# The prologue of a clustered attention and MoE kernel: the first head pair's masks built head by head

## The chip, the cores and the metric

The kernel runs on one core of one Trainium2 chip. The metric is the device time of one execution in microseconds. The profile is that of one execution, by the hardware profiler.

## The reference

Three parts follow one another: an attention in which a query sees only the keys of its own cluster, a dense MLP, and a mixture of experts with a skip rule. The change lies in the attention, in its first microseconds.

```python
B, H, S, D = 2, 8, 768, 64                 # centroids: (8, 16, 64)
q_n, k_n, c_n = (t / (norm(t) + 1e-6) for t in (q, k, centroids))
q_assign = argmax(einsum('bhsd,hcd->bhsc', q_n, c_n), -1)
k_assign = argmax(einsum('bhsd,hcd->bhsc', k_n, c_n), -1)
mask = q_assign[..., :, None] == k_assign[..., None, :]
scores = where(mask, q @ k.T / sqrt(D), -1e9)
attn = softmax(scores) @ v                  # (2, 8, 768, 64)
x = attn as (1536, 512); h = x @ w_in; x = max(0.01 * h, h) @ w_out
# then: top-1 expert of 8 for each token with x @ w_skip > 0, added to x
```

## The kernel before

**Tiling.** The 16 heads are worked on as 8 pairs (`p`), two heads side by side in the 128 partitions. A pair takes 12 steps `s` of the main loop: 6 query tiles of 128 for each of 2 heads; even steps are head 0, odd steps head 1. In a step, `st_scores` makes a 128x768 score tile on TensorE (tile `sps`) and takes its row maximum on VectorE (`st`); `st_exp` takes the exponential on ScalarE (`pr`); three steps later `st_transpose` and `st_evac` turn the tile (`tps`, evicted to `pt` by ScalarE, L435); later still `st_av` multiplies by v. Score tiles use a PSUM tag S of two buffers.

**Precision and masks.** A score is a sum of two pairs of matmuls (L371). q and k are split into a rounded `hi` part and a rest `lo`. For head 0, tile `UA` holds hi in rows 0 to 63 and the one-hot cluster of each query (times a big constant, minus it) and key in rows 64 to 79; it is used with 80 rows. Tile `VA` holds a second arrangement of hi and lo in 128 rows. Head 1 has `UB` and `VB`. Each tile has a q half (index 0) and a k half (index 1). Since the transposed pair has head 1 in partitions 64 to 127, and V needs hi and lo across the halves, parts of U and V are copied between partitions by DMA, 192 KB each ("exchange" transfers).

**Prologue (pair 0).** `load_qk(0)` loads q, the centroids (`cnat`, L107) and k, and `load_qk(1)` the next pair, all on SyncE's queue (SP). `first_copy(i)` regroups a half of q or k, one head on ScalarE (L475), the other on VectorE for q (L477) and GpSimd (POOL) for k (L479). `prep_centroids` normalises the centroids on VectorE into `cexp`; `prep_cblk` transposes them (L164). `raw_pe` transposes q and k (L179) and `raw_act` evicts them (L191). `first_hi` makes hi: q on POOL (L199), k on ScalarE (L197); `first_lo` makes lo on VectorE (L497). Then come the exchange transfers of pair 0: L502 to L505 (hi), L509 (head 1's lo of q, read from VA rows 64 to 127 of the q half), L510 (on POOL's queue), L514 and L515 (lo of k), and last

```python
nc.sync.dma_start(Yq[0:64], Xq[64:128])     # L509: VB <- VA
...
nc.sync.dma_start(Xq[64:128], Uq[0:64])     # L516: VA <- UA, over the rows that L509 reads
```

`assign_pe` multiplies by the centroids (`asps`, L232), `assign_act` evicts (`sc`, L238), `argmax_pe` transposes the scores of both heads, q and k, into one tile of 128x384 (`scps`, L244). `argmax_0` to `argmax_3` are five VectorE operations on that whole tile (L251, L256, L259, L264, L269) that end in the one-hot `oh`. Then `raw_pe` and `raw_act` of pair 1 are issued, and `mask_first(0)` and `mask_first(1)`: 12 transposes of `oh` each (`mps`, L280), k's part evicted by ScalarE (L283), q's by VectorE (L286). `split_first(1, i)` (POOL, L208 and L209) and its DMAs follow, then the loop.

**Order.** The schedule is written by hand: each engine executes in the order in which the program issues to it, and the framework adds the semaphores. A DMA waits on its queue's engine before it is issued, and holds what stands behind it there.

Of the kernel before, what the change touches and what calls it, by code (L numbers as in the profile page):

```python
# [8 lines left out]
F32 = mybir.dt.float32  # L9
F32R = mybir.dt.float32r  # L10
F16 = mybir.dt.float16
BF16 = mybir.dt.bfloat16
I32 = mybir.dt.int32
U32 = mybir.dt.uint32
AF = mybir.ActivationFunctionType
# [10 lines left out]
def kernel(  # L26
# [42 lines left out]
    def ps_s(name):  # L69
        return psum.tile([P, 2, 512], F32, tag="S", name=name, bufs=2)  # L70
# [4 lines left out]
    def ps_a(shape, name, dt=F32):  # L75
        return psum.tile(shape, dt, tag="A", name=name, bufs=1)
# [16 lines left out]
    def load_qk(p):  # L93
        b, cc = divmod(p, NPAIR)
        for nm, src in (("q", q), ("k", k)):
            if p:
                t = att_a.tile([P, NT, 2, D], F32, tag="nat" + nm, name="nat" + nm)
                nat[nm, p] = t
                nc.sync.dma_start(t, src[b, 2 * cc:2 * cc + 2].rearrange("h (p t) d -> p t h d", t=NT))
            else:  # L100
                t = att.tile([P, 2, HS], F32R, tag="pr", name="first", bufs=4)
                t = _f(t.rearrange("p a b -> p (a b)")).rearrange("p (h t d) -> p h t d", h=2, d=D)
                nc.sync.dma_start(t, src[b, 0:2].rearrange("h (p t) d -> p h t d", t=NT))
                first[nm] = t
                nat[nm, 0] = nat0[:, "qk".index(nm)]
            if p == 0 and nm == "q":
                nc.sync.dma_start(cnat, centroids.rearrange("h c d -> (h c) d"))  # L107

    def load_v(p):
        b, cc = divmod(p, NPAIR)  # L110
# [51 lines left out]
    def prep_cblk():  # L162
        cps = ps_s("cps")[:, 0, 0:P]
        nc.tensor.transpose(cps, cexp.rearrange("p h d -> p (h d)"), ident)  # L164
        nc.vector.tensor_copy(cblk.rearrange("p a b -> p (a b)"), cps)
# [5 lines left out]
    def raw_pe(p, i):  # L171
        if i == 0:
            raw_t[p] = att_a.tile([P, 4, HS], F32, tag="raw", name="raw")
            uv_t[p] = tuple(att_a.tile([P, 2, S], F32R, tag=n, name=n, bufs=2) for n in ("UA", "UB", "VA", "VB"))
        qk, half = divmod(i, 2)
        src = nat["qk"[qk], p]
        ps = ((ps_t, ps_t, ps_m, ps_a)[i] if p == 0 else ((ps_t, ps_t, ps_a, ps_t)[i] if p == 1 else ps_m))([P, 3, P], "rawps")
        for j in range(3):
            nc.tensor.transpose(ps[:, j, :], src[:, 3 * half + j].rearrange("p h d -> p (h d)"), ident)  # L179
        ps_prep["raw", i] = ps  # L180
# [89 lines left out]
                                op=ALU.is_equal)  # L270
        oh_t[p] = oh

    def mask_first(h):
        U = uv_t[0][h]
        for qk in (1, 0):
            ps = (ps_m if h else ps_t)([P, S], "mps", BF16) if qk or not h else ps_a([P, S], "mps", BF16)
            for i in range(2):
                for j in range(3):
                    o = (3 * i + j) * P
                    nc.tensor.transpose(ps[64:64 + NC_, o:o + P], oh_t[0][:, j, 4 * qk + 2 * i + h, :], identb)  # L280
            ps = ps[64:64 + NC_, :]
            if qk:
                nc.scalar.activation(out=U[64:64 + NC_, 1, :], in_=ps, func=AF.Copy)  # L283
            else:
                for cs in (slice(0, HS), slice(HS, S)) if h == 0 else (slice(0, S),):
                    nc.vector.tensor_scalar(out=U[64:64 + NC_, 0, cs], in0=ps[:, cs], scalar1=BIG, scalar2=-BIG,  # L286
                                            op0=ALU.mult, op1=ALU.add)

    def mask_pe(p):
        ps = ps_m([P, 3, P], "ohps", BF16)  # L290
# [178 lines left out]
    def first_copy(i):  # L469
        nm = "qk"[i // 2]  # L470
        ts_ = slice(3 * (i % 2), 3 * (i % 2) + 3)
        for h in range(2):
            src, dst = first[nm][:, h, ts_, :], nat[nm, 0][:, ts_, h, :]
            if h:
                nc.scalar.activation(out=dst, in_=src, func=AF.Copy)  # L475
            elif nm == "q":
                nc.vector.tensor_copy(dst, src)  # L477
            else:
                nc.gpsimd.tensor_scalar(out=dst, in0=src, scalar1=1.0, scalar2=1.0, op0=ALU.mult, op1=ALU.mult)  # L479

    first_copy(0)
    prep_centroids()
    first_copy(2)
# [10 lines left out]
    def first_lo(qk, halves=(0, 1)):  # L494
        for half in halves:
            cs = slice(half * HS, (half + 1) * HS)
            nc.vector.tensor_tensor(out=lo_k[:, half, :] if qk else VA[:, 0, cs], in0=raw_t[0][:, 2 * qk + half, :],  # L497
                                    in1=_f(UA[:, qk, cs]), op=ALU.subtract)
# [6 lines left out]
    nc.sync.dma_start(Yk[0:64], Uk[64:128])  # L505
    first_lo(0, (0,))
    prep_cblk()
    first_lo(0, (1,))
    nc.sync.dma_start(Yq[0:64], Xq[64:128])  # L509
    nc.gpsimd.dma_start(Xk[0:64], Uk[0:64])  # L510
    assign_pe(0)
    first_lo(1)
    lo_kf = _f(lo_k.rearrange("p a b -> p (a b)"))
    nc.sync.dma_start(Xk[64:128], lo_kf[0:64])  # L514
# [2 lines left out]
    prep(0, 3, "a0")  # L517
    nc.scalar.activation(out=warm, in_=warm, func=AF.Exp)
    prep(0, 3, "pb")
    for r in range(4, 7):  # L520
        for slot in ("d", "pb"):
            prep(0, r, slot)
    load_v(0)
    for i in range(4):
        raw_pe(1, i)
        raw_act(1, i)
    load_qk(2)
    mask_first(0)
    mask_first(1)
    for i in range(4):  # L530
        split_first(1, i)

# [149 lines left out]
    def conv_ops(n, a, b):  # L682
        if 0 <= n < len(pieces):
            for i_ in range(a, b):
                convert_op(*pieces[n], i_)
            if b == 5:
                load_next(n + 5)

    for s in range(NSTEP + 12 + LAG):
        p, r = divmod(s, 12)  # L690
        if s < NSTEP:
            st_scores(s)
        conv_step(s, 0)
        preps(p, r, "a0")
        preps(p, r, "pa")
        if 0 <= s - LAG < NSTEP:
            st_transpose(s - LAG)
            st_evac(s - LAG)
        gf, rf = divmod(s, 6)
        if 0 < gf <= NSTEP // 6:  # L700
            if rf == 3:
                recip_rows(gf - 1)
            elif rf == 4:
                nc.sync.dma_start(rscr[gf - 1], rrow_t.pop(gf - 1))
        g, kt = divmod(s - 6 - LAG, 6)
        if 0 <= g < NSTEP // 6 and kt % 2:
            st_av(g, kt - 1)
            st_av(g, kt)
        if s < NSTEP:
            st_exp(s)  # L710
        if 0 <= g < NSTEP // 6 and kt == NT - 1:
            av_evac(g)
            av_split(g)
        if 0 <= g < NSTEP // 6 and kt == 3:
            recip_load(g)
        if 0 < gf <= NSTEP // 6 and rf < 2:
            recip(gf - 1, rf)
        preps(p, r, "d")
        preps(p, r, "pb")
        if r == 10 and p + 1 < NP:  # L720
            load_v(p + 1)
        conv_step(s, 1)
        if s == NSTEP:
            att_a.release()
            rt = pool("rt", "left")
            ring_b[0] = pool("ring_b", "left")
            wip[0] = pool("wi", "left")
            for c in range(NDIR // 4, NPC // 4):
                load_f32(c)
            load_next(2)  # L730
        if s == NSTEP + 4:
            for i in range(3):
                split_i(i)
# [848 lines left out]
```

## Time and profile before

| | us |
|---|---|
| median of 3 runs | 661.1 (661.08 to 661.39) |
| the profiled execution | 660.89 |
| its span in the trace | 659.2 |
| first matmul in the trace | 4.41 |
| first score matmuls | 18.08 |

The profile's times count from the start of the span. "Busy" is time in which an engine executes; what stands in brackets behind an instruction is how long its engine was idle before it and what ended the wait. The chain of waits follows from the last instruction back to what released it each time. A row "x4" merges instructions of one kind that follow each other.

### The profile page before, as it was taken

To read this page: it belongs to the slowest core of one execution; us is meant where nothing else is said; L and a number is where in the kernel's file an instruction comes from. 1 tells how busy PE (TensorE), PEld (TensorE's weight loads), DVE (VectorE), ACT (ScalarE), POOL (GpSimd) and SP (SyncE) were. 2 spreads that over 40 slices of the span, in tenths; PEclk is the share of its full clock that TensorE was granted. 3 is DMA by queue.
4 is the path that set the end of the run, shared out by engine and by line. 5 is a ranking of instruction groups with operands and counts; after the bars stand their busy time and mean duration, and the time that the engine had idled before them with its cause. 6 is when DMAs were issued, how large, how long until landed. Compare 5 with 4: busy or idle time off the path is not lost.

```text
span 659.2 us, 10058 instructions
## 1 busy us (share of the span) xinstructions
PE 632.9 (96%) x3599; PEld 489.3 (74%) x3599; DVE 437.8 (66%) x767; ACT 422.5 (64%) x829; POOL 164.2 (25%) x215
## 2 busy tenths in 40 slices
PE   5999989999999999999999999999999999999995
PEld 4766666766776765888888888888888878688874
DVE  6756668686768663898865335645556548999962
ACT  5887787988888886655454444444654356688860
POOL 4234636463727324400000000000000025004211
PEclk9999999999999999999999999999999999999998
DMA  8865655667675617232104000006145337999930
GB/s 193 202 175 144 157 142 150 171 185 191 182 193 137 181 46 271 75 125 95 34 1 167 25 0 1 1 0 256 39 155 190 138 128 254 365 369 366 372 133 27
DMA packets 63636, 99.53 MB, mean 151 GB/s; under 512 B 27697, under 2 KB 31763, under 8 KB 63200
## 3 DMA queue, kind: packets, MB, share of 16 engines
q1 hardware_dynamic: 60304, 90.62, 44.1%
q0 software_dynamic: 3280, 8.24, 3.8%
q8 instruction: 29, 0.48, 0.3%
q14 instruction: 23, 0.19, 0.1%
HBM read 72.73 MB, written 12.70 MB: 130 GB/s over the span
## 4 chain that ended last, share of the span: by engine, by line
PE 87%; ACT 6%; DVE 3%; issue 2%; POOL 2%; DMA 0%; POOLq 0%
PE ups L669 20%; PE acc L775 19%; PE sps L371 9%; PE avps L443 9%; PE hps L1273 7%; PE yps L1304 7%; PE tps L428 7%; ACT pr L389 2%; ACT pt L435 2%; DVE st L374 1%; PE hT L1285 1%; PE acc L1165 1%; PE x2T L859 1%; PE rawps L179 1%; PE asps L232 1%
## 5 line engine op out<-in xcount | busy, mean ns | idle before, releaser
L374 DVE TENSOR_REDUCE st<-sps 128x1 f32<-128x768 f32 x96 | 91.7, 955 | 69.0 <-PE sps L371 68.5
L435 ACT ACTIVATE pt<-tps 128x384 f32<-128x384 f32 x192 | 84.6, 501 | 25.8 <-PE tps L428 25.0
L389 ACT ACTIVATE pr<-sps,st 128x768 f32<-128x768 f32 x96 | 87.2, 909 | 10.9 <-DVE st L374 10.3
L428 PE MATMUL tps<-ident,pr 128*128 128x128 f32 x576 | 78.6, 272 | 0.5 <-ACT pt L435 0.5
L669 PE MATMUL ups<-xh,whii 128*128 128x512 f32 x192 | 74.8, 390 | 0.0
L669 PE MATMUL ups<-xh,wloi 128*128 128x512 f32 x192 | 74.7, 389 | 0.0
L669 PE MATMUL ups<-xl,whii 128*128 128x512 f32 x192 | 74.7, 389 | 0.0
L775 PE MATMUL acc<-whio,gh 128*128 128x512 f32 x183 | 73.0, 399 | 0.0
L443 PE MATMUL avps<-pt,vnat 128*64 128x384 f32 x384 | 72.1, 498 | 0.0
L428 PEld LDWEIGHTS tps<-ident,pr 128*128 128x128 f32 x576 | 68.2, 140 | 5.1 <-ACT pt L435 1.6
L775 PE MATMUL acc<-whio,gl 128*128 128x512 f32 x183 | 71.4, 390 | 0.0
L775 PE MATMUL acc<-wloo,gh 128*128 128x512 f32 x183 | 71.3, 390 | 0.0
L760 ACT ACTIVATE gh<-g 128x512 fp32r<-128x512 f32 x48 | 30.4, 633 | 43.6 <-DVE g L759 43.6
L758 ACT ACTIVATE lk<-ups 128x512 f32<-128x512 f32 x48 | 28.4, 592 | 37.3 <-PE ups L669 30.8
L759 DVE TENSOR_TENSOR g<-ups,lk 128x512 f32<-128x512 f32 x48 | 33.0, 688 | 28.7 <-ACT lk L758 28.6
L762 DVE TENSOR_TENSOR gl<-g,gh 128x512 fp32r<-128x512 f32 x48 | 33.3, 693 | 25.2 <-ACT gh L760 25.2
L1013 POOL DMA_INDIRECT xe<-x_scratch,eix x1 | 1.2, 1165 | 190.0 <-DVE eix L1012 190.0
L646 DVE TENSOR_TENSOR wloi<-rawb,whii 128x512 fp32r<-128x512 f32 x36 | 24.7, 686 | 27.5 <-ACT whii L645 27.4
L443 PEld LDWEIGHTS avps<-pt,vnat 128*64 128x64 f32 x384 | 23.4, 136 | 25.6 <-issue 25.5
L669 PEld LDWEIGHTS ups<-xh,whii 128*128 128x128 f32 x192 | 36.0, 188 | 8.1 <-issue 0.6
L669 PEld LDWEIGHTS ups<-xl,whii 128*128 128x128 f32 x192 | 36.1, 188 | 7.5
L669 PEld LDWEIGHTS ups<-xh,wloi 128*128 128x128 f32 x192 | 36.0, 188 | 7.4
(303 smaller groups left out, 1350.1 us busy)
## 6 DMA issues: line engine op xcount, KB each, us to landing
rawb<-in_moe_w_dram SPq DMA_DIRECT2D x25, 1024.0 KB
rawa<-in_moe_w_dram SPq DMA_DIRECT2D x10, 1024.0 KB
stg<-in_moe_w_in_dram SPq DMA_DIRECT2D x16, 512.0 KB
stg<-in_moe_w_out_dram SPq DMA_DIRECT2D x16, 512.0 KB
UB<-UA SPq DMA_DIRECT2D x16, 192.0 KB
vnat<-in_v_dram SPq DMA_DIRECT2D x8, 384.0 KB
rb<-recip_scratch POOLq DMA_DIRECT2D x32, 96.0 KB, 2.9
w_f_scratch<-cvt SPq DMA_DIRECT2D x12, 256.0 KB
```

Source lines behind the costliest of these rows:

```text
L371: nc.tensor.matmul(ps[:, kh, 0:HS], lhsT=t[0:n, 0, qs], rhs=t[0:n, 1, kh * HS:(kh + 1) * HS], start=first, stop=not first)
L374: nc.vector.tensor_reduce(out=st[:, 0:1], in_=ps[:, :, 0:HS], axis=AX.XY, op=ALU.max, negate=True)
L389: nc.scalar.activation(out=pr, in_=ps[:, :, 0:HS], func=AF.Exp, bias=st[:, 0:1], accum_out=sm_t[g][:, 3 * h + j:3 * h + j + 1])
L428: nc.tensor.transpose(ps[:, t, :], pr[:, kh, t * P:(t + 1) * P], ident)
L435: nc.scalar.activation(out=pt[:, 3 * kh:3 * kh + 3, j, :], in_=t_t[s][kh], func=AF.Copy)
L443: nc.tensor.matmul(av_t[g][64 * h:64 * h + 64, :], lhsT=vnat[p][:, h, kt, :], rhs=pt_t[p, half, h][:, kt].rearrange("p j c -> p (j c)"), s ...
L669: nc.tensor.matmul(ps, lhsT=w[:, cc, :], rhs=x[:, blk, cc, :], start=(n == 0), stop=(n == 3 * KD - 1))
L759: nc.vector.tensor_tensor(out=g, in0=ps, in1=t, op=ALU.max)
L762: nc.vector.tensor_tensor(out=gl, in0=g, in1=_f(gh), op=ALU.subtract)
L775: nc.tensor.matmul(ps, lhsT=a[:, ts_], rhs=w, start=(fc == 0 and n == 0), stop=(fc == NFC - 1 and n == 2))
L1273: nc.tensor.matmul(ps, lhsT=x[:, c, :], rhs=w, start=(n == 0), stop=(n == len(mm) - 1))
L1304: nc.tensor.matmul(ps[:, cs], lhsT=x[:, f, :], rhs=w[:, cs], start=(h == 0 and f == 0 and n == 0), stop=(h == 1 and f == 3 and n == 2))
```

## The change

1. The centroids' DMA moves from SyncE's to ScalarE's queue. 2. Of q's `first_copy`, the second half's head 0 moves from VectorE to POOL. 3. Eight identity matmuls (128x128, into a score buffer that is not read) are issued to TensorE: five first of all, one after the centroid transpose, two after the assignment. 4. The five argmax operations run head by head on half the elements (`argmax_first`), and head 0's all stand before the rest; head 1's first two stand before head 0's masks, the other three behind its first tile. 5. `mask_first` is split in three: the 12 transposes of a head; k's eviction, half on ScalarE and half on VectorE; q's eviction in pieces of 128, 256 and 384 queries. Head 0's transposes, k's eviction and q's first 128 queries come before the loop's first step; head 1's transposes and evictions stand after `st_scores(0)`; the other pieces of q follow in steps 0 to 3. 6. `raw_act(1, 2)` and `(1, 3)` stand behind head 0's k eviction, and pair 1's fourth transposed tile goes to a score buffer.

```diff
-                nc.sync.dma_start(cnat, centroids.rearrange("h c d -> (h c) d"))
+                nc.scalar.dma_start(cnat, centroids.rearrange("h c d -> (h c) d"))
...
+        if p == 1 and i == 3:
+            ps = ps_s("rawps")[:, 0, 0:HS].rearrange("p (j c) -> p j c", c=P)
...
+    def argmax_first(h, i):
+        V = nc.vector
+        sc = by_head(ps_prep["am"], h)
+        sh = [P, 3, 4, NC_]
+        if i == 0:
+            am0["m", h] = att_a.tile([P, 3, 4], F32, tag="mx0", name="mx0", bufs=2)
+            V.tensor_reduce(out=am0["m", h], in_=sc, axis=AX.X, op=ALU.max)
...
+    def mask_first_pe(h):
         for qk in (1, 0):
-            ps = (ps_m if h else ps_t)([P, S], "mps", BF16) if qk or not h else ps_a([P, S], "mps", BF16)
+            ps = (ps_t if h == 0 else ps_m if qk else ps_a)([P, S], "mps", BF16)
...
+    def mask_first_k(h):
+        U, ps = uv_t[0][h], mf_t[h, 1]
+        nc.scalar.activation(out=U[64:64 + NC_, 1, 0:HS], in_=ps[:, 0:HS], func=AF.Copy)
+        nc.vector.tensor_copy(U[64:64 + NC_, 1, HS:S], ps[:, HS:S])
+
+    def mask_first_q(h, a, z):
+        U, ps = uv_t[0][h], mf_t[h, 0]
+        nc.vector.tensor_scalar(out=U[64:64 + NC_, 0, a:z], in0=ps[:, a:z], scalar1=BIG, scalar2=-BIG,
+                                op0=ALU.mult, op1=ALU.add)
...
-            elif nm == "q":
+            elif i == 0:
                 nc.vector.tensor_copy(dst, src)
...
+    wps = ps_s("wps")[:, 0, 0:P]
+
+    def warm_pe(n):
+        for _ in range(n):
+            nc.tensor.matmul(wps, lhsT=ident, rhs=ident, start=True, stop=True)
+
+    warm_pe(5)
     first_copy(0)
...
     prep_cblk()
+    warm_pe(1)
     first_lo(0, (1,))
...
     assign_pe(0)
+    warm_pe(2)
...
-    for r in range(4, 7):
-        for slot in ("d", "pb"):
-            prep(0, r, slot)
+    for i in range(5):
+        argmax_first(0, i)
     load_v(0)
     for i in range(4):
         raw_pe(1, i)
-        raw_act(1, i)
+    raw_act(1, 0)
+    raw_act(1, 1)
     load_qk(2)
-    mask_first(0)
-    mask_first(1)
+    argmax_first(1, 0)
+    argmax_first(1, 1)
+    mask_first_pe(0)
+    mask_first_k(0)
+    raw_act(1, 2)
+    raw_act(1, 3)
+    mask_first_q(0, 0, P)
+    for i in range(2, 5):
+        argmax_first(1, i)
...
+    st_scores(0)
+    mask_first_pe(1)
+    mask_first_k(1)
+    mask_first_q(1, 0, P)
+    mask_first_q(0, P, HS)
     for s in range(NSTEP + 12 + LAG):
         p, r = divmod(s, 12)
-        if s < NSTEP:
+        if 0 < s < NSTEP:
             st_scores(s)
+        if 0 < s < 4:
+            mask_first_q(s % 2, P if s == 1 else HS, HS if s == 1 else S)
```

## Rows read from the trace of the kernel before

**Rows 1.** The page: TensorE's busy time, its granted clock in slices.

```profile
...
PE 632.9 (96%) x3599; PEld 489.3 (74%) x3599; DVE 437.8 (66%) x767; ACT 422.5 (64%) x829; POOL 164.2 (25%) x215
...
PEclk9999999999999999999999999999999999999998
...
```

**Rows 2.** The chain of waits of 0 to 45 us: start us, us, what.

```profile
...
8.69 1.57 PE asps L232 x8
...
11.76 0.57 DVE mx L251
...
14.13 1.25 DVE oh L269
...
15.42 2.73 PE mps L280 x24
18.15 1.08 PE sps L371 x4
...
```

**Rows 3.** Timeline of SyncE's DMA queue: start us, us to issue.

```profile
...
1.31 0.46 SPq L107 DMA_DIRECT2D cnat<-in_centroids_dram  x1
1.81 0.43 SPq L103 DMA_DIRECT2D first<-in_k_dram  x1
...
7.97 0.55 SPq L502 DMA_DIRECT2D UB<-UA  x1
...
15.64 0.46 SPq L516 DMA_DIRECT2D VA<-UA  x1
...
```

**Rows 4.** Waits of SyncE's queue: total us, times, longest.

```profile
...
SPq L516 <- DMA VB<-VA: 1.8, 1, 1.8
...
```

**Rows 5.** DMA packets: 9.0-16.4, 16.4-17.8, 17.4-17.6 us.

```profile
...
DMA packets 601, 1.57 MB, mean 213 GB/s; under 512 B 121, under 2 KB 121, under 8 KB 601
...
DMA packets 90, 0.21 MB, mean 150 GB/s; under 512 B 17, under 2 KB 26, under 8 KB 90
...
DMA packets 12, 0.04 MB, mean 184 GB/s; under 512 B 0, under 2 KB 0, under 8 KB 12
...
```

**Rows 6.** TensorE's timeline, 3 to 35 us (PEld: weight loads).

```profile
...
4.41 1.52 PE L179 MATMUL rawps<-ident,nat 128*128 128x128 f32 x6 [4.41 <-DVE csq L146]
...
18.53 0.36 PEld L371 LDWEIGHTS sps<-VA 128*128 128x128 f32 x2
...
19.24 0.59 PE L371 MATMUL sps<-UB 80*128 80x384 f32 x2
...
20.12 0.85 PE L232 MATMUL asps<-raw,cblk 128*32 128x384 f32 x8
21.29 0.62 PE L371 MATMUL sps<-UA 80*128 80x384 f32 x2 [0.32 <-ACT pr L389]
...
34.65 0.33 PE L406 MATMUL rcps<-ident,rc 128*128 128x128 f32 x1 [0.39 <-ACT pt L435]
...
```

**Rows 7.** VectorE's timeline, 3 to 24 us.

```profile
...
16.90 1.03 DVE L286 TENSOR_SCALAR UA<-mps 16x384 fp32r<-16x384 bf16 x2 [1.54 <-PE mps L280]
18.18 0.95 DVE L286 TENSOR_SCALAR UB<-mps 16x768 fp32r<-16x768 bf16 x1 [0.25 <-PE mps L280]
19.25 1.93 DVE L374 TENSOR_REDUCE st<-sps 128x1 f32<-128x768 f32 x2
...
23.92 0.96 DVE L374 TENSOR_REDUCE st<-sps 128x1 f32<-128x768 f32 x1 [0.67 <-PE sps L371]
```

**Rows 8.** Windows, 24-26 us: busy PE, PEld, DVE, ACT, POOL.

```profile
...
24.00:26.00 2.00, 1.97 (x15) 1.65 (x13) 2.00 (x3) 2.00 (x7) 0.00 (x0) 1.00 0.39 93
...
```

**Rows 9.** ScalarE's timeline, 3 to 26 us.

```profile
...
5.88 0.62 ACT L475 ACTIVATE nat<-first 128x192 f32<-128x192 f32 x2 [1.00 <-DMA first<-in_k_dram]
6.41 1.39 ACT L191 ACTIVATE raw<-rawps 128x384 f32<-128x384 f32 x3
...
22.11 0.48 ACT L238 ACTIVATE sc<-asps 128x384 f32<-128x384 f32 x1
...
24.25 0.87 ACT L435 ACTIVATE pt<-tps 128x384 f32<-128x384 f32 x2
...
```

More of the change, by code (lines that the diff above doesn't have):

```diff
@@ L176, in raw_pe @@
         src = nat["qk"[qk], p]
-        ps = ((ps_t, ps_t, ps_m, ps_a)[i] if p == 0 else ((ps_t, ps_t, ps_a, ps_t)[i] if p == 1 else ps_m))([P, 3, P], "rawps")
+        if p == 1 and i == 3:
+            ps = ps_s("rawps")[:, 0, 0:HS].rearrange("p (j c) -> p j c", c=P)
+        else:
+            ps = ((ps_t, ps_t, ps_m, ps_a)[i] if p == 0 else ((ps_t, ps_t, ps_a)[i] if p == 1 else ps_m))([P, 3, P], "rawps")
         for j in range(3):
@@ L271, in argmax_3, with by_head @@
         oh_t[p] = oh
-    def mask_first(h):
-        U = uv_t[0][h]
+    def by_head(ap, h):
+        return ap.rearrange("p j (a h) c -> p j a h c", h=2)[:, :, :, h, :]
+    am0 = {}
+    def argmax_first(h, i):
[5 more added lines that the diff above has]
+            V.tensor_reduce(out=am0["m", h], in_=sc, axis=AX.X, op=ALU.max)
+        elif i == 1:
+            if "e" not in am0:
+                am0["e"] = att_a.tile([P, 3, 8, NC_], F32, tag="eq", name="eq")
+                oh_t[0] = att_a.tile([P, 3, 8, NC_], BF16, tag="oh", name="oh")
+            V.tensor_tensor(out=by_head(am0["e"], h), in0=sc, in1=am0["m", h].unsqueeze(3).to_broadcast(sh),
+                            op=ALU.is_equal)
+        elif i == 2:
+            eq = by_head(am0["e"], h)
+            V.tensor_tensor(out=eq, in0=eq, in1=cw[:, 0:4].unsqueeze(1).to_broadcast(sh), op=ALU.mult)
+        elif i == 3:
+            V.tensor_reduce(out=am0["m", h], in_=by_head(am0["e"], h), axis=AX.X, op=ALU.max)
+        else:
+            V.tensor_tensor(out=by_head(oh_t[0], h), in0=by_head(am0["e"], h),
+                            in1=am0["m", h].unsqueeze(3).to_broadcast(sh), op=ALU.is_equal)
+    mf_t = {}
+    def mask_first_pe(h):
         for qk in (1, 0):
-            ps = (ps_m if h else ps_t)([P, S], "mps", BF16) if qk or not h else ps_a([P, S], "mps", BF16)
+            ps = (ps_t if h == 0 else ps_m if qk else ps_a)([P, S], "mps", BF16)
             for i in range(2):
@@ L280, in mask_first @@
                     nc.tensor.transpose(ps[64:64 + NC_, o:o + P], oh_t[0][:, j, 4 * qk + 2 * i + h, :], identb)
[L281 to L287, printed above, removed]
+            mf_t[h, qk] = ps[64:64 + NC_, :]
+    def mask_first_k(h):
[6 more added lines that the diff above has]
+                                op0=ALU.mult, op1=ALU.add)
     def mask_pe(p):
```

## Prediction

> **What bounds the kernel now.** I read the page first. TensorE is busy 96% of the span [rows 1], so almost anything before or beside it is free, and only the few microseconds before the attention loop runs steadily can be won or lost. The diff touches only that prologue, so I read the chain of waits of the first 45 us next [rows 2]. The reader is to see one dependent line: the input load, the centroid scaling on DVE, the assignment matmuls, five argmax operations on DVE (11.76 to 15.38), 24 mask transposes, and the first score matmuls at 18.15. The change shortens the part from the argmax to the first scores.
>
> A chain shows only what ended last. So I asked of each operand of the first scores when it was there. They are two pairs of matmuls in one accumulation: UA (80 rows, mask included), then VA (128 rows, the exchanged hi and lo parts, no mask). VA's second half of q is filled by the transfer of L516. SP issues it only at 15.64 [rows 3], after waiting 1.8 us for the transfer of L509, which reads the same rows of VA [rows 4]. In front stand eight exchange transfers of 64 rows x 3072 B: 480 of their 512 packets pass between 9.0 and 16.4 (601 less the 121 under 2 KB) without a gap (1.57 MB at 213 GB/s, so 0.92 us each) [rows 5]. L516's own 64 packets (90 less the 26 under 2 KB) pass between 16.4 and 17.8, the last ones after 17.4 [rows 5]. VA's weight load starts at 18.53 [rows 6]. So VA became complete somewhere between 17.8 and 18.53, while DVE had head 0's mask done at 17.93 [rows 7]. Two lines end within half a microsecond of each other; the change speeds up one. I take 18.53 as the moment at which VA allows its load, because the load starts there behind a U pair that started at 18.15.
>
> After the first steps ScalarE is the bound: it is busy 2.00 of 2.00 us from 24 to 26 (DVE too, there alone) [rows 8], and TensorE last waits for it at 34.65 [rows 6]. From there TensorE is packed. A shift of the point where ScalarE becomes packed thus reaches the end at full size.
>
> **The change part by part.**
>
> Centroids on ScalarE's queue: SP loses one issue: 1.31 to 1.81, 0.50 us [rows 3]. The k load and all SP issues behind it (two loads of the next pair, then the exchange transfers) move up. ScalarE issues one DMA ahead of its table load, in time in which it has nothing to do until 3.9. What follows k: ScalarE waits 1.00 us for it at 5.88, copies (0.62), then evicts q's transposes (6.41) [rows 9]; POOL rounds q's two halves; L502 issues at 7.97 [rows 3]; then come the eight packed transfers, L509, L516. All of it moves by a shift s. Bounds: 0 if k's landing is set by bytes and not by its issue; 1.00 if ScalarE's whole wait goes. I take s = 0.5, the slot that is taken out of SP's line.
>
> The Trainium skill (DMA: Bandwidth & Descriptors, Issuing engines are not separate DMA queues) says that DMAs of all issuers run on the same 16 engines, and that another issuer saves only the issue time. By that, s is the 0.50 us slot, the value taken above, and +1.2 us in the end; by the reading that the whole 1.00 us wait goes, the end would be +0.7.
>
> Identity matmuls: Five go where TensorE is idle until 4.41 [rows 6]. Nearest rows for one: a transpose, 1.52 / 6 = 0.25; a quarter of the assignment, 1.57 / 4 = 0.39 for three times the columns. At most 0.4 each, 2.0 for five: hidden. One stands between the centroid transpose and the assignment and two between the assignment and the argmax transposes: up to 1.2 together, less 0.5 that ScalarE's copy takes there anyway. If they raise the clock early, TensorE's parts ahead of the scores shorten: the assignment takes 1.57 at 8.69 and 0.85 at 20.12 [rows 2, 6]. The granted clock reads full all along [rows 1], but these durations say that the early stretch ran at the lower of the two levels. Either way I cost them at nothing: L516 covers it. Without that cover they are worth +0.7 to -1.7 (0.7 in the assignment, 0.3 in the argmax transposes, 0.7 in half of the mask's).
>
> Second q copy from DVE to POOL, k's mask copy split over ScalarE and DVE, the fourth raw tile in another bank: all ahead of L516's landing for head 0, so nothing.
>
> Head by head: Five operations on 192 instead of 384 elements: between half and all of 0.57 [rows 2], I take 0.38 each. Head 0's one-hot is ready at about 11.76 + 1.9 = 13.7 instead of 15.38. Twelve transposes instead of 24 (2.73, so 1.4) and the copies give a UA ready at about 15.5. The first U pair then runs at 15.5 instead of 18.15, and TensorE stands: the V pair must wait for L516, at 18.53 - 0.5 = 18.03. The wait that is removed is replaced by another one.
>
> Now what is queued behind. On TensorE, head 1's twelve mask transposes are issued after the first scores, so they cannot start before about 18.5. On DVE, head 1's k copy and q tile stand behind the first maximum. Before, all of head 1 was finished at 18.18 + 0.95 = 19.13 [rows 7], while the first scores ran. So the first maximum starts at 19.25 - 0.5 = 18.75 and, 0.97 long, ends at 19.72 [rows 7]. Head 1's transposes run in its shadow: 12 x 0.1 from 18.6, done by 19.7. DVE: k's half, 384 columns: 1.03 / 2 = 0.5 [rows 7]: 20.2. Then q's first 128 columns: 768 take 0.95, 384 take 0.5, so 0.24: 20.45 [rows 7]. Step 1's scores start at 20.48 instead of 19.24 [rows 6]: 1.24 late. Its maximum and exponential are then 1.2 late. ScalarE's copy of pair 1's assignment (22.11) stands behind that exponential [rows 9], the argmax transposes behind the copy, step 3's scores behind those on TensorE, and step 0's probability transposes behind these. So the eviction at 24.25 [rows 9], with which ScalarE becomes packed, is 1.2 late. The rest of the q masks, three DVE operations of 0.3 to 0.5 in steps 1 to 3, fit into its gaps in steps 1 and 2. In step 3 DVE goes from the maximum (23.92) straight into other work; 0 to 0.3 more. I take 0.
>
> Sum: 1.74 - s = 1.24, less a rounding: +1.2 us. Bounds: s = 1.0 gives +0.7; s = 0 gives +1.7, with DVE's 0.3 +2.0. The profiled execution took 660.89 us, 1.7 more than its span; with 1.2 that is 662.1. The median of the runs, 661.1, lies 0.2 above that execution: 662.3.
>
> **The rivals.** About 1.3 us, 0.2%, is what a measurement of this kernel can tell from no change.
>
> Faster, because the V parts are not what ends last: Then the first U and V pairs run at 15.5, the first maximum starts behind head 1's three last argmax operations (3 x 0.38 from 15.5) at about 16.6, and step 1's scores at 16.6 + 0.97 + 0.5 + 0.24 = 18.3, 0.9 before 19.24: 660.2. For it: no view shows a wait of the V load. Against: twelve of L516's 64 packets still pass between 17.4 and 17.6 [rows 5], and nothing of the change shortens eight packed transfers. The point from which it decides: step 1 comes as before if the V load can start at 18.53 - 1.74 = 16.8, which asks s = 1.7; the rows allow 1.0.
>
> Faster by more, by the clock: Here the identity matmuls bring the higher level before the assignment, and the masks, again not the transfers, set the end. Up to 1.7 more comes off; I take half, since ScalarE's copy and DVE's argmax stand between and keep their length: 659.4. For it: 1.57 against 0.85 for the same assignment. Against: as above. The Trainium skill (TensorE: Matmul & The Clock Gate, What's actually happening) says that the array starts throttled and that activity releases it; by that rule the filled gap would raise the clock earlier. The trace agrees that the early stretch is slow.
>
> No change, because the delay is absorbed: Step 1 is late but step 2 was waiting for a score buffer before (its scores at 21.29 stood behind an exponential [rows 6]), and the exponential of step 0 is now early by 0.5. If ScalarE takes up the slack, the end moves by 0 to 0.3: 661.3. Against: ScalarE's assignment copy and TensorE's order tie step 3 to step 1, as above.
>
> **How the numbers follow.** Forecast, the delay carried: 0.60, of it 0.29 below +1.3 and 0.31 above. V parts not last: 0.16, of it 0.06 beyond -1.3. Clock: 0.11, all beyond. Absorbed: 0.13. Faster 0.06 + 0.11 = 0.17; same 0.29 + 0.10 + 0.13 = 0.52; slower 0.31. The forecast's own range is 661.8 to 663.1. The range goes down to 660.0 to take in absorption and most of the first rival; left out are the clock case and tails, under 0.2.
>
> **What the profile after would show.** Right: the first U pair near 15.5 and the V pair two microseconds later, with TensorE idle between; L516's issue near 15.1; L502's near 7.5; head 1's mask transposes after the first V pair; step 1's scores near 20.5; ScalarE packed from about 25.4. The centroid slot right: k's issue at 1.3. The clock part: an assignment of 0.85 instead of 1.57 that moves nothing. Wrong would be: a V pair directly behind the U pair before 16.8, or step 1's scores before 19.2. It would also be wrong if L516's landing were free to move by more than the slot, for example by exchange transfers that go faster than 0.92 us once the input loads end earlier.

## The result and the profile after

The changed kernel takes 666.3 us (median of 4 runs, 665.61 to 666.72) against 661.3 for the kernel before (median of 4, one more than above): ratio 1.0071, 95% interval 1.0059 to 1.0083. By the ratio, which the text goes by, it is 4.7 us (0.0071 x 661.3) slower; the medians differ by 5.0. The forecast was 662.3 in a range of 660.0 to 663.1: right in sign, and in the mechanism that it names, but four times too small. The profiled execution took 665.61 us, span 663.8.

TensorE's timeline of the changed kernel:

```profile
8.88 0.85 PE L235 MATMUL asps<-raw,cblk 128*32 128x384 f32 x8 [0.25 <-DVE cblk L165]
...
13.06 0.84 PE L311 MATMUL mps<-identb,oh 128*16 128x128 bf16 x12 [0.85 <-DVE oh L300]
15.81 0.59 PE L406 MATMUL sps<-UA 80*128 80x384 f32 x2 [1.91 <-ACT raw L194]
18.20 0.91 PE L406 MATMUL sps<-VA 128*128 128x384 f32 x2 [1.80 <-DMA VA<-UA]
19.04 1.45 PE L311 MATMUL mps<-identb,oh 128*16 128x128 bf16 x12
21.26 0.98 PE L406 MATMUL sps<-UB 80*128 80x384 f32 x2 [0.77 <-issue]
...
22.81 1.51 PE L235 MATMUL asps<-raw,cblk 128*32 128x384 f32 x8
...
266.10 0.50 PE L720 MATMUL ups<-xh,whii 128*128 128x512 f32 x1
...
275.07 0.50 PE L833 MATMUL acc<-whio,gh 128*128 128x512 f32 x1 [0.50 <-DVE g L817]
```

The first score pair runs at 15.81, 2.3 us earlier than before; then TensorE stands for 1.80 us, until the transfer VA<-UA has landed, and the V pair starts at 18.20. Head 1's transposes follow it, and step 1's scores come at 21.26 instead of 19.24 [rows 6]. The first assignment (pair 0's) takes 0.85 us; in the kernel before it took 1.57 in the chain [rows 2], which is 1.51 in TensorE's timeline. The second (pair 1's), at 22.81, takes 1.51 instead of 0.85 [rows 6].

SyncE's queue of the changed kernel:

```profile
1.31 0.46 SPq L103 DMA_DIRECT2D first<-in_k_dram  x1
...
7.63 0.55 SPq L544 DMA_DIRECT2D UB<-UA  x1
...
15.30 0.46 SPq L560 DMA_DIRECT2D VA<-UA  x1
```

k is issued 0.50 us earlier, the exchange transfers only 0.34 (7.97 and 15.64 before [rows 3]): s is 0.34.

Windows of the changed kernel (busy PE, PEld, DVE, ACT, POOL; then granted clock, DMA share, GB/s):

```profile
15.50:18.00 2.50, 0.59 (x2) 0.30 (x2) 1.68 (x4) 0.27 (x1) 2.33 (x4) 1.00 0.77 166
18.00:20.00 2.00, 1.80 (x12) 1.39 (x13) 0.85 (x1) 0.11 (x1) 0.73 (x1) 0.57 1.13 307
20.00:25.00 5.00, 4.23 (x19) 2.30 (x17) 2.58 (x6) 2.45 (x6) 0.00 (x0) 0.50 0.90 209
25.00:30.00 5.00, 4.71 (x30) 3.97 (x30) 4.25 (x6) 3.65 (x9) 0.00 (x0) 0.99 0.64 165
```

After the new idle time (1.91 us ahead of 15.81, 1.80 ahead of 18.20) the granted clock reads 0.57 from 18 to 20 us and 0.50, the lower level, from 20 to 25. That is why everything from the V pair to the second assignment takes nearly twice as long.

ScalarE's exponentials, the kernel before and the changed kernel:

```profile
20.24 0.90 ACT L389 ACTIVATE pr<-sps,st 128x768 f32<-128x768 f32 x1 [1.90 <-DVE st L374]
...
21.22 0.90 ACT L389 ACTIVATE pr<-sps,st 128x768 f32<-128x768 f32 x1
...
23.29 0.90 ACT L389 ACTIVATE pr<-sps,st 128x768 f32<-128x768 f32 x1 [0.70 <-DVE st L374]
```

```profile
14.39 0.48 ACT L316 ACTIVATE UA<-mps 16x384 fp32r<-16x384 bf16 x1 [1.81 <-DMA VB<-UA]
...
19.89 0.48 ACT L316 ACTIVATE UB<-mps 16x384 fp32r<-16x384 bf16 x1 [4.12 <-PE mps L311]
20.39 0.90 ACT L424 ACTIVATE pr<-sps,st 128x768 f32<-128x768 f32 x1
...
23.91 0.90 ACT L424 ACTIVATE pr<-sps,st 128x768 f32<-128x768 f32 x1 [2.53 <-DVE st L409]
...
26.64 0.90 ACT L424 ACTIVATE pr<-sps,st 128x768 f32<-128x768 f32 x1 [1.35 <-DVE st L409]
```

VectorE's timeline of the changed kernel:

```profile
14.90 0.56 DVE L317 CAST UA<-mps 16x384 fp32r<-16x384 bf16 x1 [1.24 <-ACT UA L316]
15.39 0.28 DVE L321 TENSOR_SCALAR UA<-mps 16x128 fp32r<-16x128 bf16 x1
...
19.15 0.96 DVE L409 TENSOR_REDUCE st<-sps 128x1 f32<-128x768 f32 x1 [1.87 <-PE sps L406]
20.40 0.56 DVE L317 CAST UB<-mps 16x384 fp32r<-16x384 bf16 x1 [0.29 <-ACT UB L316]
20.88 0.28 DVE L321 TENSOR_SCALAR UB<-mps 16x128 fp32r<-16x128 bf16 x1
...
26.63 0.56 DVE L321 TENSOR_SCALAR UA<-mps 16x384 fp32r<-16x384 bf16 x1
```

Read side by side, the lag behind the kernel before grows in stages: exponential of step 0 +0.15, step 1 +2.69 (23.91 - 21.22), step 2 +3.35, the first up projection of the MLP +3.85 (266.10 against 262.25), its first down projection +4.51 (275.07 against 270.56), the span +4.6. So something beyond the forecast happens in steps 1 to 4, and something more 250 us after the changed code. TensorE's timeline of the kernel before, in the stretch of the second:

```profile
262.25 0.50 PE L669 MATMUL ups<-xh,whii 128*128 128x512 f32 x1
...
267.84 0.39 PE L669 MATMUL ups<-xh,whii 128*128 128x512 f32 x1
268.07 0.39 PE L669 MATMUL ups<-xl,whii 128*128 128x512 f32 x1
...
270.56 0.39 PE L775 MATMUL acc<-whio,gh 128*128 128x512 f32 x1
```

There the up projections follow one another without a gap and the first down projection stands directly behind them; in the changed kernel it waits 0.50 us for VectorE's `g`.

### The profile page after: what moved, and what is told of

The parts are those of the page before. It is cut to its first block, busy times and chain, and to the rows that moved or that the text cites. A ratio compares the mean times of both kernels' runs of the same rounds, so it can differ in the third digit from the quotient of the medians.

```text
span 663.8 us, 10100 instructions
## 1 busy us (share of the span) xinstructions
PE 635.8 (96%) x3615; PEld 491.2 (74%) x3615; DVE 440.6 (66%) x776; ACT 422.0 (64%) x829; POOL 164.0 (25%) x216
## 4 chain that ended last, share of the span: by engine, by line
PE 85%; ACT 6%; DVE 2%; issue 2%; DMA 2%; POOL 2%; SPq 0%; POOLq 0%; ACTq 0%
PE acc L833 19%; PE ups L720 19%; PE avps L478 9%; PE sps L406 9%; PE hps L1331 7%; PE yps L1362 7%; PE tps L463 6%; ACT pr L424 2%; ACT pt L470 2%; PE rawps L182 1%; DVE st L409 1%; PE hT L1343 1%; PE acc L1223 1%; PE x2T L917 1%; PE asps L235 1%
```

## The experiments

Ratios are to the kernel before on the same chip (medians 661.4 to 661.6). Not all runs were on one chip, so runs are compared by their ratios. "Fillers" are further identity matmuls in TensorE's gaps.

| run | us | ratio, 95% interval |
|---|---|---|
| e1 centroid queue alone | 661.9 | 1.0004 [0.9994, 1.0013] |
| e2 identity matmuls alone | 666.8 | 1.0079 [1.0062, 1.0096] |
| e3 head 1's masks between the pairs | 664.0 | 1.0038 [1.0024, 1.0052] |
| e4 gaps filled | 664.5 | 1.0044 [1.0027, 1.0061] |
| e5 both of these | 663.0 | 1.0024 [1.0015, 1.0034] |
| e6 PSUM places of before | 665.4 | 1.0058 [1.0040, 1.0076] |
| e7 e2 with PSUM places of before | 661.5 | 0.9998 [0.9988, 1.0008] |
| e8 transfer into V early | 664.5 | 1.0042 [1.0027, 1.0057] |
| e9 e5 with PSUM places of before | 662.4 | 1.0015 [1.0006, 1.0024] |
| e10 e9, head 0's q columns early | 661.9 | 1.0005 [0.9996, 1.0014] |
| e11 e10, k by one engine | 661.3 | 0.9997 [0.9988, 1.0006] |
| e12 e11, V early | 661.9 | 1.0006 [0.9997, 1.0015] |
| e13 e11, head 1's q columns in one piece | 660.9 | 0.9992 [0.9983, 1.0001] |
| e14 e13, V early with GpSimd | 662.5 | 1.0020 [1.0011, 1.0029] |
| e15 e11 without fillers | 662.5 | 1.0015 [1.0006, 1.0024] |
| e16 e13, V early, rest later | 660.6 | 0.9988 [0.9979, 0.9998] |
| e17 e13, centroids on SyncE's queue | 661.0 | 0.9996 [0.9987, 1.0005] |
| e18 e16 with five fillers | 660.0 | 0.9977 [0.9968, 0.9986] |

**e1: the kernel before with the queue move alone.**

```diff
-                nc.sync.dma_start(cnat, ...)
+                nc.scalar.dma_start(cnat, ...)
```

> The kernel before with the centroids' DMA on ScalarE's queue and nothing else. Theory of the order (head 1's masks queued behind the late V operands made the changed kernel slow): this part is small either way; k lands 0.4 us earlier but q, sharing the engines with the centroids, 0.5 later, so -0.3 to +0.5 us against the kernel before, V's last transfer issued 0.3 earlier. Rival (the queue move itself costs time, because q lands late): +0.5 to +1.5 us. Theory of the clock: no difference.

No measurable change. The slot is real (L516 issues at 15.21 instead of 15.64), but nothing of it is seen in the time. Two things in this profile bear on the clock. Its first assignment took 0.85 us, although it has no identity matmuls; and the granted clock fell to 0.57 from 14 to 18 us, with no loss in this execution (661.10).

**e2: the kernel before with the eight identity matmuls alone.**

```diff
+    wps = ps_s("wps")[:, 0, 0:P]
+    warm_pe(5)        # and warm_pe(1), warm_pe(2), where the change has them
```

> The kernel before with the eight identity matmuls and nothing else. Theory of the order: the assignment takes 0.85 us and head masks are ready 1 to 1.5 us earlier, but the first V pair still waits for its transfer until about 18.4, so 0 to -0.5 us against the kernel before. Theory of the clock as a gain: -1 to -1.7 us. If the identity matmuls are what makes the changed kernel slow (clock raised early, then dropped): +1 to +3 us and a granted clock of 0.5 somewhere between 15 and 25 us.

5.2 us slower: the part that was costed at nothing loses, alone, as much as the whole change. Its first assignment took 1.51 us, not the 0.85 that was expected. Its attention is 0.2 us late (first up projection 262.48); the rest arises in the MLP. TensorE's timeline of e2:

```profile
267.81 0.39 PE L678 MATMUL ups<-xh,wloi 128*128 128x512 f32 x1
271.46 0.79 PE L678 MATMUL ups<-xh,whii 128*128 128x512 f32 x1 [3.27 <-DVE g L768]
272.05 0.63 PE L678 MATMUL ups<-xl,whii 128*128 128x512 f32 x1
```

After two up projections (of 12 matmuls each) TensorE stands 3.27 us, then runs at 0.63 instead of 0.39 us a matmul: the clock fell there too (granted 0.50 from 271 to 277 us). In the kernel before, the third follows at once. `wps` is an allocation of the PSUM tag S ahead of all others; it changes the place of the tags and which of S's two buffers each later step uses. The first two up projections are still made in a buffer of tag S; the MLP's own PSUM pool is opened where these tiles lay.

**e3: head 1's masks between step 0's two pairs.**

```diff
+    def head_1():
+        mask_first_pe(1); mask_first_k(1); mask_first_q(1, 0, P)
-    st_scores(0)
-    mask_first_pe(1); mask_first_k(1); mask_first_q(1, 0, P)
+    st_scores(0, head_1)       # called after the U pair, before the V pair
```

> The changed kernel with head 1's mask transposes and evictions issued between the first U pair and the first V pair instead of behind the V pair. Theory of the order: head 1 is ready when V lands, step 1's scores start near 19.0 instead of 21.3, and most of the loss goes: 661.5 to 663.5 us. Theory of the clock: TensorE still stands idle for 3 us before 17.3, the clock still falls at about 18.3, and less than half of the loss goes: 664 to 665.5 us.

2.2 us of the 4.7 come back: the order costs. TensorE's timeline of e3:

```profile
17.33 0.84 PE L311 MATMUL mps<-identb,oh 128*16 128x128 bf16 x12 [0.93 <-DVE oh L300]
18.17 0.98 PE L406 MATMUL sps<-VA 128*128 128x384 f32 x2
19.24 0.98 PE L406 MATMUL sps<-UB 80*128 80x384 f32 x2
```

Head 1's transposes now lie in the wait for the transfer, and step 1's scores are at 19.24, where they were before. But the score pairs still take 0.98: the clock fell here as well.

**e4: TensorE's gaps filled, order unchanged.** Twelve identity matmuls into a tile that is not read, six ahead of the U pair and six behind it.

```diff
     mask_first_pe(0)
+    fill_pe(6)
...
+    st_scores(0, lambda: fill_pe(6))
```

> The changed kernel with twelve more identity matmuls, six behind head 0's mask transposes and six between the first U pair and the first V pair, so that TensorE hardly stands idle between 13.9 and 18.2; order unchanged. Theory of the clock: the granted clock stays at 1.0 through 18 to 25 us, the first V pair takes 0.52 instead of 0.91, the second assignment 0.85 instead of 1.51, and 2 to 3 us of the loss go: 663 to 664.5 us. Theory of the order alone: the time stays within 0.7 us of the changed kernel, 665.5 us and up.

1.8 us come back (the two intervals just overlap). Windows of e4:

```profile
18.00:20.00 2.00, 1.35 (x14) 0.95 (x14) 1.12 (x2) 0.65 (x2) 0.75 (x1) 1.00 1.13 310
20.00:25.00 5.00, 3.53 (x22) 2.37 (x23) 3.82 (x7) 2.86 (x6) 0.00 (x0) 1.00 0.90 210
```

The clock is 1.00 where it was 0.57 and 0.50, and the first up projection comes 1.8 us earlier (264.27 against 266.10). So the fall is worth about 1.8 us in the changed kernel, and with the gaps filled it does not happen. TensorE's timeline of e4:

```profile
20.69 0.59 PE L406 MATMUL sps<-UB 80*128 80x384 f32 x2 [1.12 <-ACT UB L316]
```

With the clock up and the order as it was, step 1's scores start at 20.69 and its exponential at 22.67, 1.45 us later than in the kernel before; in the changed kernel it is 2.69. The forecast for this step was 20.48 and 1.2.

**e5: e3's order and nine fillers.**

```diff
+    fill_pe(6)              # behind mask_first_pe(0)
     def head_1():
+        fill_pe(3)
```

> The changed kernel with head 1's masks between the first U and V pair and nine identity matmuls in TensorE's gaps (six behind head 0's masks, three behind the first U pair). If order and clock are two separate halves of the prologue's loss (3.8 us at the steady steps; each of the two single repairs left about 2.0): 0 to 0.6 us left there, and 662 to 663 us with the 0.8 that arises at the start of the MLP. If both repairs removed the same loss: 1.5 to 2 left, 663.8 to 664.5.

Order and clock together: 3.1 of 4.7 us. 1.6 are left. Beside e4's 1.8 for the clock, that leaves 1.3 for the order where the clock stays up (the intervals of e4 and e5 overlap).

**e6: the changed kernel with four unused PSUM tiles allocated first,** so that each tag gets the place that it had.

```diff
+    for mk_ in (ps_t, ps_t, ps_m, ps_a):
+        mk_([P, P], "lay")
     wps = ps_s("wps")[:, 0, 0:P]
```

> The changed kernel with four unused PSUM tiles allocated in front of the identity matmuls' tile, so that the PSUM tags get the same places as in the kernel before; nothing else. Theory of the PSUM places (the 0.8 us that arise at the first down projection come from another bank under the first up projections): the delay stays 3.8 us through the MLP, 665.2 to 665.6 us, and no wait of the first down projection for VectorE. Rival (VectorE is late there for another reason): as the changed kernel, 666 to 666.5.

TensorE's timeline of e6:

```profile
274.46 0.39 PE L722 MATMUL ups<-xh,wloi 128*128 128x512 f32 x1
274.69 0.39 PE L835 MATMUL acc<-whio,gh 128*128 128x512 f32 x1
```

The wait of 0.50 at the first down projection is gone; its lag (274.69 - 270.56 = 4.13) is that of the attention. The medians show 0.9 us, with intervals that overlap those of the changed kernel.

**e7: e2 with those four and one more unused tile of tag S,** so that places and the turn of S's buffers are those of before.

```diff
+    ps_s("lay")             # beside the four of e6
     wps = ps_s("wps")[:, 0, 0:P]
```

> The kernel before with the eight identity matmuls and five unused PSUM tiles in front, so that places and rotation of the PSUM tags are those of the kernel before. Theory of the PSUM places: the 5.2 us that the identity matmuls alone cost go to 0 to 0.3, 661.3 to 662 us, and the third up projection follows the second directly. Rival (the clock that fell at 270 us is the matter of the identity matmuls themselves): 664 us and more.

The whole 5.2 us are gone. That shows that the identity matmuls cost by their PSUM tile, not by their time; place and turn are restored together here, so which of the two matters is not shown. The granted clock fell in this profile as well (0.50 from 16 to 22 us). This execution (662.23) is the slowest of ten, but over the ten the mean clock (0.991 to 0.997) and the time do not go together, and the median shows no loss: no cost of a fall can be measured in the order of the kernel before.

**e8: the changed kernel with the transfer into V early.** q's low part for the exchange gets a tile of its own, so that VA<-UA overwrites nothing that another transfer reads.

```diff
-    nc.sync.dma_start(Yq[0:64], Xq[64:128])
+    nc.sync.dma_start(Xq[64:128], Uq[0:64])
...
+    nc.sync.dma_start(Yq[0:64], lo_q[64:128])
-    nc.sync.dma_start(Xq[64:128], Uq[0:64])
```

> The changed kernel with head 1's lo part of q in a tile of its own (two half-height subtractions in place of one), so that V's last transfer no longer waits for another to land; it is issued sixth, and k's lo for V seventh. Theory of the late V operands: the V pair starts near 16.4 instead of 18.2, head 1's masks near 17.4, step 1's scores near 19.1 instead of 21.3, TensorE stands idle less, and 1.8 to 3 us of the loss go: 663 to 664.5 us. Rival (what the change queues on VectorE and ScalarE sets the first steps whatever V does): less than 0.7 us gained.

TensorE's timeline of e8:

```profile
9.60 1.51 PE L235 MATMUL asps<-raw,cblk 128*32 128x384 f32 x8 [0.54 <-DVE cblk L165]
...
16.93 0.59 PE L406 MATMUL sps<-UA 80*128 80x384 f32 x2 [1.12 <-ACT raw L194]
17.35 0.52 PE L406 MATMUL sps<-VA 128*128 128x384 f32 x2
18.40 0.84 PE L311 MATMUL mps<-identb,oh 128*16 128x128 bf16 x12 [0.52 <-DVE oh L300]
20.31 0.98 PE L406 MATMUL sps<-UB 80*128 80x384 f32 x2 [1.08 <-ACT UB L316]
```

The V pair follows the U pair without a wait, and yet only 1.9 us are won: head 1's masks still stand behind, and the assignment starts 0.72 us late, behind two more half-height subtractions (0.55 each). In this profile it also runs at the lower level (1.51 us), and the clock falls later on (0.50 from 22 to 26 us). So the wait for the transfer is not the whole loss; how much of it is left to the clock here is not shown.

**e9, e10, e11: what e5 leaves, one step at a time.** e9 adds e6's unused tiles to e5; e10 evicts head 0's remaining 640 q columns in one piece ahead of step 0's maximum; e11 evicts each head's k mask in one ScalarE instruction.

```diff
+    mask_first_q(0, P, S)                        # e10, ahead of st_scores(0, ...)
...
+        nc.scalar.activation(out=U[64:64 + NC_, 1, :], in_=ps, func=AF.Copy)   # e11
```

> The changed kernel with head 1's masks between step 0's two pairs, with nine identity matmuls in TensorE's gaps, and with four unused PSUM tiles ahead so that every later tile lies where it lay before. Theory: the loss is three separate things and this takes two and a half of them away; the places alone are worth 0.65 to 0.8 us, so 662.2 to 662.4 against 663.0 without them, attention 0.9 us behind the kernel before throughout and the MLP no further behind. Rival (the places were worth 0.65 only while the clock was low): 663.0, as without them.

> As the run before it, and head 0's remaining query mask columns in one piece before step 0's first maximum, in VectorE's wait for it, instead of two pieces in steps 0 and 2. Theory that the pieces on VectorE between the maxima (0.42 and 0.56 us in steps 1 to 4) delay maxima and transposes: the steady lag falls from 0.9 us to 0.3 to 0.5, time 661.7 to 662.0. Rival that the rest is the serial evacuation of head 1's key mask (0.48 us on ScalarE, then 0.56 us on VectorE): no change from the run before it, 662.3.

> As the run before it, and the key masks of each head leave PSUM in one ScalarE instruction of 768 columns, as in the kernel before. Theory that two halves one behind the other cost more than one whole (1.1 us from ScalarE's start to VectorE's end against some 0.9): 0.1 to 0.2 us from each of steps 0 and 1, time 661.5 to 661.8. Rival that the halves are free because the first maximum waits for the transfer into V: no change.

Each moves the median the expected way, by 0.5 to 0.7; neighbours' intervals overlap, so only the sum is sure: from 1.0024 to 0.9997, 1.8 us, with the intervals apart. With these losses mended, the changed kernel stands where the kernel before stood. e10's profile shows no gain: its first assignment ran at the lower level there (1.51 us).

**e12, e14, e16: the transfer into V early in the mended kernel.** e12 adds e8's edit to e11; e14 and e16 build on e13, with the subtraction of the rows that stay in V on GpSimd (e14) or on VectorE behind the low key parts (e16).

```diff
+    eng = nc.vector if a else nc.gpsimd     # e14: rows 0 to 63, which stay in V, on GpSimd
...
     first_lo(1)
+    nc.vector.tensor_tensor(out=VA[0:64, 0, :], ...)     # e16: these rows in one instruction
```

> As the run before it, and the high part's transfer into V (waited for by step 0's V pair) issued early, with the query's low part in a tile of its own. With all other losses taken out, the theory that the first step waits for that transfer until 18.1 us says that now the first exponential starts up to 1 us earlier and the kernel comes to 660.5 to 661.2, at or under the kernel before. Rival that the two extra half-height subtractions on VectorE, or the later landing of the low key parts behind it, take this back: 661.5 to 662.5.

> As e13, and the high part's transfer into V issued early, with the query's low part for the transfer in a tile of its own and the half-height subtractions for the rows that stay in V on GpSimd, so that VectorE has no more to do than before. Theory that the V pair's wait (0.74 us in e11) holds the first step: V pair at 17.6 us instead of 18.4, first exponential 0.6 to 0.8 us earlier, time 660.2 to 660.6, under the kernel before. Rival that the first maximum or the chain through the assignment takes its place: no earlier than 0.2 us, 660.9 to 661.2.

> As e13, and the high part's transfer into V issued early as in e14, with the rows of the query's low part that stay in V subtracted on VectorE in one instruction of 64 x 768 after the low key parts, so that neither the centroids nor the assignment wait for it. Theory that the V pair's wait in e13 holds the first step: V pair by 17.8 us, first exponential 0.4 to 0.7 us earlier than in e13, time 660.1 to 660.5. Rival that the extra 0.8 to 1.0 us on VectorE ahead of the first argmax passes on to the masks: no gain, 660.8 to 661.5.

e12 gains nothing: the assignment starts at 9.51 instead of 9.07, as in e8, and takes 1.51 us in this profile. e14 loses 1.8 us to e13. VectorE and GpSimd of e14:

```profile
7.58 2.03 DVE L159 TENSOR_SCALAR cexp<-cnat,cst,par 128x64 f32<-128x64 f32 x2
```

```profile
7.62 1.94 POOL L547 TENSOR_TENSOR VA<-raw,UA 64x384 fp32r<-64x384 f32 x2
```

The two scalings of the centroids take 2.03 us (0.54 in e13) and end when GpSimd's two subtractions end. The Trainium skill (SBUF — State Buffer, SBUF: two separate sides) says that VectorE, in some of its operations, and GpSimd share a port pair that one holds for a whole instruction while the other is blocked; the trace agrees, 0.54 against 2.03. e16 avoids this and gains 0.3 on e13, within the uncertainty, though its profile's chain runs through the fillers (1.53 and 0.68 us).

**e13: e11 with head 1's remaining 640 q columns in one piece in step 1.**

```diff
-            mask_first_q(1, P, HS)     # and (1, HS, S) in step 3
+            mask_first_q(1, P, S)
```

> As e11, and head 1's remaining query mask columns in one piece of 640 (0.82 us, as head 0's in e11) in step 1, where VectorE waits 0.78 us for scores, instead of 256 there and 384 in step 3. Theory that the 384 columns (0.56 us) ahead of step 4's maximum cost what the steps of e11 lose between step 3 (0.34 us ahead of the kernel before) and step 4 (0.04 us behind): the steps stay 0.25 to 0.35 us ahead, time about 661.0, 0.3 us under e11. Rival that ScalarE or the transposes hold step 4 anyway: no change from e11, 661.3.

ScalarE's exponential of step 4, e11 and then e13:

```profile
26.66 0.90 ACT L425 ACTIVATE pr<-sps,st 128x768 f32<-128x768 f32 x1 [0.23 <-DVE st L410]
```

```profile
26.19 0.94 ACT L425 ACTIVATE pr<-sps,st 128x768 f32<-128x768 f32 x1
```

0.47 us earlier, without the wait for the maximum: in these profiles the 384 columns between two maxima were the rest of the lag. From e9 to e13 the intervals are apart: the query pieces and the split k mask are worth 1.5 us.

**e15: e11 without the nine fillers.**

```diff
-    fill_pe(6)
...
-        fill_pe(3)
```

> As e11 without the nine identity matmuls in TensorE's gaps. Theory that the clock falls in the gaps between 13 and 18 us whatever the order, and that the score pairs, masks and second assignment at the lower level cost as much as in the changed kernel (1.8 us there): 662.8 to 663.2. Rival that the clock's fall mattered only because head 1's masks and the first maxima stood behind one another, and is now mostly hidden by ScalarE and VectorE: 661.4 to 662.0.

Between both theories. Its 11 times spread from 660.91 to 663.73 (e11: 660.87 to 661.90). The mean granted clock of each execution tells them apart: 0.997 and 0.998 in the three fastest (up to 661.70), 0.990 to 0.994 in the other eight (from 661.85); in e11 it is 0.995 to 0.997 in all. A lower mean says that the clock fell in that execution, not where. So the fillers remove the executions in which it falls, and the median of the eight is 2.0 us above that of the three. The profiled execution, 660.91, kept the clock with its gaps open.

**e17: e13 with the centroids on SyncE's queue again.**

```diff
-                nc.scalar.dma_start(cnat, ...)
+                nc.sync.dma_start(cnat, ...)
```

> As e13, and the centroids loaded from SyncE's queue, between q and k, as in the kernel before. If the queue move is worth its issue slot, the transfers from 7.6 us on and the V pair come 0.35 to 0.5 us later and the kernel is at 661.2 to 661.4. Rival that q, which then lands 0.55 us earlier, makes up for it: 660.7 to 661.0.

Not resolved: 661.0 against 660.9. As in e1, the queue move is worth nothing that can be measured: k is issued 0.50 us earlier, but q's first copies start at 4.46 us in the changed kernel instead of 3.91.

**e18: e16 with five fillers instead of nine.**

```diff
-    fill_pe(6)
+    fill_pe(3)
...
-        fill_pe(3)
+        fill_pe(2)
```

> As e16 with five identity matmuls in TensorE's gaps (three and two) instead of nine (six and three). Theory that in e16 the fillers themselves delay the first score pair (issued behind 1.53 us of them) and head 1's masks: both come 0.4 to 0.7 us earlier, the clock stays up, time 659.9 to 660.3. Rival that with fewer of them the clock falls in some executions, as in e15: 660.6 to 661.5 with a spread of over 2 us.

TensorE's timeline of e18:

```profile
15.65 0.58 PE L405 MATMUL sps<-UA 80*128 80x384 f32 x2 [0.21 <-issue]
...
16.73 0.83 PE L311 MATMUL mps<-identb,oh 128*16 128x128 bf16 x12
17.49 0.62 PE L405 MATMUL sps<-VA 128*128 128x384 f32 x2
18.12 0.62 PE L405 MATMUL sps<-UB 80*128 80x384 f32 x2
```

660.0 us, 1.5 us (0.14 to 0.32%) under the kernel before: the best version of the study. Against e16, which it resembles but for four fillers, the intervals overlap. Both of step 0's pairs and head 1's masks run without a wait for another engine, and step 1's scores are at 18.12 instead of 19.24.

## Why the prediction was right or wrong

**Right: the wait that is replaced.** The U pair came at 15.81 (forecast 15.5), L516 at 15.30 (15.1), the V pair at 18.20 (18.03), head 1's transposes behind it. s was 0.34, not 0.5. U was 0.3 late because ScalarE's k mask waited until 14.39 for a transfer that still read UA, which the forecast had not looked at, and VectorE's half (14.90) and first q piece (15.39) follow it. (The profile puts the U pair's wait down to ScalarE's eviction `raw`, which ended then; in e11 the U pair starts before that eviction has ended.) That costs nothing, since the V pair waits longer. The order behind the wait costs: 2.2 us in e3, and about 1.3 where the clock stays up (e4 against e5). So the term that the forecast is made of, 1.2, is of the right size; what it lacks are the terms that it put at nothing.

**Wrong: "Either way I cost them at nothing: L516 covers it".** This step failed, in two ways. First the clock. The forecast weighed an early rise, and the profile has one (0.85 at 8.88), though e1 and e2 do not tie it to the identity matmuls (0.85 without them, 1.51 with them). But the forecast gave TensorE's stretch after the new idle time the durations of the kernel before: "12 x 0.1 from 18.6" took 1.45 (0.84 in e4), step 1's U pair 0.98 instead of 0.59. The forecast itself has TensorE stand there, from the U pair to the V pair, and did not price that. e4 shows 1.8 us for it. The Trainium skill (TensorE: Matmul & The Clock Gate, HAM oscillation — how this bites in real kernels) says that long waits of TensorE for a transfer bring the lower rate back and that this is paid each time; the trace agrees that idle time goes before the fall (0.50 from 20 to 25 us, 1.00 with the gaps filled), but only the second of the two idle stretches here ends with a transfer. The forecast had weighed the clock for a gain only.

Second, the tile. "the fourth raw tile in another bank: all ahead of L516's landing for head 0, so nothing" and, for `wps`, nothing but the time of its matmuls: a new PSUM allocation moved the places and the turns of the tags, and the MLP waits 0.50 us at 275 (3.27 in e2). e7 shows that this is all of e2's loss; in the changed kernel it is 0.6 to 0.9 us (e6, and e9 against e5; both pairs of intervals overlap, but in both profiles the wait is gone). How the MLP's pool maps its banks onto the older tiles is argued from the code, not seen in a row.

**Wrong: "0 to 0.3 more. I take 0"** for the query pieces on VectorE, and the split k copy at nothing for head 0. The two halves run one after the other: VectorE's waits for ScalarE's (20.40, behind 19.89 + 0.48), although the columns are different. The pieces stand in front of maxima in steps 1 to 4. With places settled, e13 shows 1.5 us for both.

**Misread, without harm: "TensorE last waits for it at 34.65".** Waits of the kernel before, whole execution (us in total, times, longest):

```profile
PE rcps L406 <- ACT pt L435: 6.9, 15, 1.0
```

TensorE waits for ScalarE 14 more times in the attention. What was concluded from it held all the same: the lag at the first of these waits, 3.77 us (38.42 against 34.65), reaches the first up projection as 3.85.

**The sum.** Forecast +1.2. Measured terms, from the ratios: clock 1.8, order 1.3 beside it (2.2 where the clock is left to fall; together 3.1), places 0.6 to 0.9, pieces and halves about 1.5: 5.2 to 5.5 against 4.7 measured. The changed kernel with all of these mended (e13) is 0.5 us under the kernel before, which accounts for the difference and which its interval does not tell from none.

**The rivals.** "V parts not last" is out: V was last. The clock case had an early rise right and the sign wrong. Absorption did not happen: no slack took up the delay of step 1.

## What to carry to other kernels

When a change opens a gap on TensorE, cost what follows the gap at the lower clock as well as at the higher one, as long as no row shows which it is, and ask whether other ready work (here head 1's masks) can stand in the gap. Count a new PSUM tile as a change to every later phase: look at what the next pool's first matmuls wait for, and keep the places with unused tiles if need be. When one operand is made early, find for each other operand and for all that is queued behind what comes last next.

## What was not expected of the hardware

A clock that was up for the assignment at 8.88 fell after two idle stretches of TensorE of 1.91 and 1.80 us, with twelve transposes and a score pair before and between them, and the windows show it back only from 25 us on, though TensorE was busy 4.23 of the 5 us before. When the clock first rises differs between profiled executions of nearly the same prologue: the same first assignment took 0.85 us in the changed kernel, e13 and e18, and 1.51 in e8, e12 and e15. The identity matmuls do not decide it: e1, without them, has 0.85, and e2, with them, 1.51. In the profiles with fillers e4, e5, e9, e11, e13 and e18 the clock rose early and stayed up; without fillers it rose early and fell again in the changed kernel, e1, e3, e6 and e7, rose late and fell in e8, and rose late and stayed up in the kernel before and e15. (In e14 it fell at 12 us, ahead of the fillers.) So open gaps alone do not bring it down; why they do so in some executions is left open. The granted clock in the windows reads 1.00 in this early stretch in both cases, so there the durations have to be read, not the column.
